# Bucketed attention and a gated MLP on one core: the penalty of unequal buckets from bits and their complements instead of one-hot columns, with the first batch planned anew

## The chip, the core and the metric

The kernel runs on one core of a Trainium2 chip. A core has TensorE (PE, with its weight loads shown as PEld), VectorE (DVE), ScalarE (ACT), GpSimd (POOL) and SyncE (SP), which here issues all DMAs. The metric is the device time of one execution in microseconds. Three runs of the kernel before took 945.35, 940.81 and 940.45 us; their median, 940.81 us, is the time before.

## The reference

Attention over 4 batches, 8 heads, 768 positions and 64 dimensions, in which a query sees only the keys of its own hash bucket, and then a gated MLP without a nonlinearity:

```python
q_bits = (np.einsum('bhsd,dk->bhsk', q, proj) > 0).astype(np.int64)      # proj is 64 x 6
k_bits = (np.einsum('bhsd,dk->bhsk', k, proj) > 0).astype(np.int64)
powers = 2 ** np.arange(n_bits)
q_bucket = np.sum(q_bits * powers, axis=-1)                               # 0 to 63
k_bucket = np.sum(k_bits * powers, axis=-1)
mask = q_bucket[:, :, :, None] == k_bucket[:, :, None, :]
scores = np.where(mask, scale * np.matmul(q, k.transpose(0, 1, 3, 2)), -1e9)
attn = np.exp(scores - np.max(scores, axis=-1, keepdims=True))
attn = attn / (np.sum(attn, axis=-1, keepdims=True) + 1e-09)
x = np.matmul(attn, v) as rows of 512 (8 heads x 64), 3072 rows in all
out = (x @ w_a) * (x @ w_b) @ w_out                                       # 512 -> 1536 -> 512
```

## The kernel before

All matmuls of values run on pairs of 16-bit parts: a number is split into a high part and a remainder, and a product is the sum of three products of parts.

**The blocks of K and Q.** `split` (line 377) prepares one block: K of a pair of heads (12 groups of 128 positions, 16 blocks in all, 4 per batch) or Q of four heads and a third of the positions (8 groups, 24 blocks, 6 per batch). It scales the block, makes the high part (L344 on ACT or L346 on DVE) and the remainder (L402, DVE), which go into tile `pt[0]` (`kt`, `qt`) and through a DMA transpose (L409) into half 1 of the transposed tile `trk` or `trq`. The high part is copied into tile `pt[1]` (L337). PE multiplies the transposed block with `proj` in two parts (L421, 12 columns per group), ACT copies one part out as `neg` (L439), and DVE compares the other with it, which gives six bits per position (L442). A scan (L443) makes the bucket's number from the six bits by Horner's rule. POOL subtracts the number from a table `buckets` of 0 to 63 (L451), and DVE compares the 64 differences with zero (L459): for Q a column holds 2^15 where the number is equal and else 0, for K −2^15 where it is not equal and else 0. The second transpose (L467) brings `pt[1]`, 64 columns of the high part and 64 of these, into half 0.

**Scores.** For each tile of 128 queries and one head, `scores` (L752) adds two products of 128 rows into two blocks of 384 keys: half 0 of Q with half 0 of K, and half 1 with half 1. The 64 one-hot rows add 0 where the buckets are equal and −2^30 where they are not. There are 192 such tiles. DVE takes the maximum (L772) and two small steps (L779, L783), ACT the exponential with its sum (L792), ACT or DVE cast it to 16 bits (L337, into `a`), POOL (or, for tiles whose key is below `BOTH_LO`, DVE) makes the remainder (L340), a DMA transpose (L812) gives `at`, and PE multiplies it with V in 18 matmuls (L821). After eight tiles DVE divides by the sums (L852, tile `x`), and the result is transposed into `xT`, in the first unit by PE (L887) and L893, L896.

**The MLP.** A unit is 256 positions of a batch, 12 units in all. For each of 12 blocks f of 128 of the 1536 columns PE does 24 matmuls (L932, `ab`), ACT scales one half (L947, `a`), DVE multiplies the other with it (L955, `g`), ACT and POOL split the product (L962, L965), and PE does six matmuls with `w_out` (L975, `o`).

**The weights.** They are loaded as 32-bit words and put together anew for 16-bit use, in the first quarter of the run: two ACT steps (L506, L514), one DVE step (L524, `raw_w` or `wo_y`), a cast to the high part (L337 on ACT or DVE), and a remainder (L340 on DVE or POOL) into `wab` or `wo`. A group of weights also needs its maximum (L546) and a scale (L569 to L577).

**The order.** `Plan` records every operation with its engines, an estimated duration, a key, and what it reads and writes. `issue` (line 138) walks through time with these estimates, gives each free engine the ready operation with the least key, chooses the engine where two are allowed, and so writes each engine's order, which is then fixed: an engine does its instructions in that order, each as soon as what it needs is there. Keys count tiles of scores. Those of the first batch are numbers of a table (`FIRST_K`, `FIRST_Q`, `FIRST_V`, `FIRST_X`, `FIRST_W` and so on, lines 45 to 51), those of later ones follow from leads and lags (lines 52 to 54). A tag of buffers limits how many of its tiles live at a time: `two` has 8 tiles (`NTWO`), of which at most two are `pt[0]`, two `pt[1]`, four hold `a`, and one `x2`.

Of the kernel before, what the change touches and what calls it, by code (L numbers as in the profile page):

```python
# [44 lines left out]
FIRST_K = (-16.3, -2.05, -0.08, 1.27)  # L45
FIRST_Q = (-9.7, 0.61)
FIRST_V = (-20.84, -4.29, 0.05, 2.68)
FIRST_X = -16.49
FIRST_W = (5.89, 12.41, 13.69, -22.11, -8.59, 22.86)
FIRST_WO = (6.46, 13.88, 17.5, 26.83, 32.86, -20.47)  # L50
FIRST_M = (20.33, 2.62)
K_LEAD, K_STEP, Q_LEAD, V_LEAD, V_STEP, X_LAG = 7.99, -2.55, 6.99, 5.66, 5.82, 11.54
BOTH_LO = 12.62
M_LAG, E_LEAD, O_LAG = 5.88, 13.29, 3.51
# [9 lines left out]
def constants():  # L64


    c = np.zeros((P, P + NK * NBITS), np.float32)
    c[:, :P] = np.eye(P)
    c[:, P:] = np.tile([0.0] + [2.0] * (NBITS - 1), NK)
    return c, np.tile(np.arange(NBUCK), (P, 1)).astype(np.float16)  # L70

# [166 lines left out]
def attention_moe(ctx: ExitStack, tc: tile.TileContext, q, k, v, proj, w_a, w_b, w_out, cst, cst_w, out):  # L238
# [43 lines left out]
    csb = cp.tile([P, P + NK * NBITS], F32, tag="csb", name="csb")  # L282
    ident = csb[:, :P]
    horner = csb[:, P:]
    buckets = cp.tile([P, NBUCK], F16, tag="buckets", name="buckets")
# [90 lines left out]

    def split(raw, x, n, side, b, key, toks, tag, fast):

# [62 lines left out]
        def numbers():  # L441
            nc.vector.tensor_tensor(out=six(bits), in0=cols(0), in1=six(neg), op=ALU.is_gt)  # L442
            nc.vector.tensor_tensor_scan(  # L443
                out=neg.t[:, :nb], data0=horner[:, :nb], data1=bits.t[:, :nb], initial=0.0,
                op0=ALU.mult, op1=ALU.add,
            )

        op("DVE", 0.6, numbers, key, r=[psb, neg, "csb"], w=[bits, neg], sbuf=True)
        op(
            "POOL", 0.2 + 1.7e-3 * size,  # L450
            lambda: nc.gpsimd.tensor_tensor(  # L451
                out=hot(), in0=buckets.unsqueeze(1).to_broadcast([P, n, NBUCK]),
                in1=six(neg)[:, :, NBITS - 1 :].to_broadcast([P, n, NBUCK]), op=ALU.subtract,
            ),
            key, r=[neg, "buckets"], w=[(pt[1], "hot")],
        )
        op(
            "DVE", 0.18 + 0.25e-3 * size,
            lambda: nc.vector.tensor_scalar(  # L459
# [604 lines left out]
```

## Time and profile before

| | us |
|---|---|
| median of three runs | 940.81 |
| lowest, highest run | 940.45, 945.35 |
| profiled execution, its own time | 945.47 |
| its span, first to last instruction | 943.7 |
| busy in the span: PE, PEld | 863.1, 695.1 |
| busy: DVE, ACT, POOL | 617.9, 607.9, 521.1 |
| DMA: 152.10 MB | 161 GB/s in the mean |

A row of the profile names the line, the engine, the operation and what is written and read (`mx<-s`: a tile `mx` from a tile `s`; buffer numbers are left out). "x192" is the count of instructions. "Busy" is time in which an engine executes; waiting, semaphores and the issuing of DMAs are not counted. The granted clock is the share of TensorE's full clock that it was given in a stretch. The share of the DMA engines is their busy time by the length of the stretch, with transfers that overlap counted apart, so that it can pass 1.

### The profile page before, as it was taken

The page shows a single profiled execution, that of the slowest core. Times are in us where ns is not written, and L with a number is a line of the kernel's source. Part 1 is how long each engine was busy: PE and PEld are TensorE (multiplying, and loading weights), DVE is VectorE, ACT ScalarE, POOL GpSimd, SP SyncE. Part 2 cuts the span into 40 slices and gives each one's busy share as a digit, 9 for nine tenths or more (in the row PEclk, how much of TensorE's full clock was granted, in tenths as well). Part 3 has the DMA queues.
Part 4 walks back from the last instruction along what each step waited for, and adds up shares of the span by engine and source line. Part 5 has one row for each costly group of instructions (what it writes and reads, how often), then busy time and mean ns, then how long its engine had stood idle before and what let it go on. Part 6 is the DMA issues. An engine that isn't in the chain of part 4 may idle for free.

```text
span 943.7 us, 23025 instructions
## 1 busy us (share of the span) xinstructions
PE 863.1 (91%) x9025; PEld 695.1 (74%) x9025; DVE 617.9 (65%) x1508; ACT 607.9 (64%) x1161; POOL 521.1 (55%) x400
## 2 busy tenths in 40 slices
PE   1356578899999999999999999999999999999998
PEld 0234456678888888888888888887888888888886
DVE  5999987978676666557776665567667665543111
ACT  5788678786765766656765776657765766654221
POOL 0345454686756566656666666656565756654111
PEclk9997588999999999999999999999999999999999
DMA  8999989589999687868997787879876777654000
GB/s 264 287 209 231 263 228 201 119 158 223 186 186 167 133 155 173 142 147 183 172 209 142 129 183 144 141 152 190 191 179 112 158 154 136 140 115 88 12 24 23
DMA packets 455725, 152.10 MB, mean 161 GB/s; under 512 B 427328, under 2 KB 447936, under 8 KB 455616
## 3 DMA queue, kind: packets, MB, share of 16 engines
q1 hardware_dynamic: 455616, 150.64, 76.4%
q8 instruction: 70, 1.15, 0.5%
q14 instruction: 39, 0.32, 0.1%
HBM read 37.87 MB, written 6.29 MB: 47 GB/s over the span
## 4 chain that ended last, share of the span: by engine, by line
PE 82%; DVE 9%; DMA 4%; issue 2%; ACT 1%; POOL 1%; SPq 1%; DVEq 0%; ACTq 0%; POOLq 0%
PE ab L932 39%; PE o L975 20%; PE s L752 11%; PE av L821 10%; DMA at<-a 2%; DVE mx L772 2%; DMA raw_w<-in_moe_w_a_dram 1%; DVE raw_w L524 1%; DVE wo_y L524 1%; DMA trq<-qt 1%; DVE wmx L546 0%; DVE wo L340 0%; ACT e L792 0%; DVE wab L340 0%; DVE sc L779 0%
## 5 line engine op out<-in xcount | busy, mean ns | idle before, releaser
L340 POOL TENSOR_TENSOR a<-e,a 128x768 f16<-128x768 f32 x188 | 323.7, 1723 | 204.7 <-ACT a L337 117.4
L932 PE MATMUL ab<-xT,wab 128*128 128x256 f16 x3456 | 418.9, 276 | 5.5 <-DVE g L955 5.4
L932 PEld LDWEIGHTS <-wab 128*128 128x128 f16 x3456 | 332.3, 99 | 64.1 <-issue 17.7
L772 DVE TENSOR_REDUCE mx<-s 128x1 f32<-128x768 f32 x192 | 182.9, 953 | 114.7 <-PE s L752 112.6
L792 ACT ACTIVATE e<-s,bias,sc 128x768 f32<-128x768 f32 x192 | 189.9, 989 | 100.0 <-DVE bias L783 90.7
L975 PE MATMUL o<-wo,g 128*128 128x512 f32 x864 | 237.6, 411 | 0.0
L965 POOL TENSOR_TENSOR g<-g,g 128x256 fp32r<-128x256 f32 x144 | 114.1, 792 | 121.1 <-ACT g L962 119.9
L975 PEld LDWEIGHTS o<-wo,g 128*128 128x128 f32 x864 | 154.6, 189 | 30.0
L752 PE MATMUL s<-trk,trq 128*128 128x384 f16 x768 | 162.8, 343 | 14.9 <-DMA trq<-qt 7.0
L821 PEld LDWEIGHTS <-at 128*128 128x128 f16 x3456 | 127.3, 100 | 42.6 <-DMA at<-a 20.4
L821 PE MATMUL av<-vh,at 128*128 128x64 f16 x2304 | 133.9, 196 | 15.9 <-DMA at<-a 13.1
L955 DVE SCALAR_TENSOR_TENSOR g<-ab,absc,a 128x256 f32<-128x256 f32 x144 | 69.0, 479 | 120.5 <-ACT a L947 75.3
L947 ACT ACTIVATE a<-ab,absc 128x256 f32<-128x256 f32 x144 | 68.2, 473 | 110.9 <-PE ab L932 106.8
L752 PEld LDWEIGHTS <-trq 128*128 128x128 f16 x768 | 70.5, 102 | 60.8 <-issue 25.9
L337 ACT CAST a<-e 128x768 f16<-128x768 f32 x137 | 113.3, 827 | 1.6
L962 ACT CAST g<-g 128x256 fp32r<-128x256 f32 x144 | 58.2, 404 | 60.8 <-DVE g L955 50.7
L821 PE MATMUL av<-vl,at 128*128 128x64 f16 x1152 | 67.3, 196 | 0.0
L451 POOL TENSOR_TENSOR kt<-buckets,neg_k 128x768 f16<-128x768 f16 x16 | 25.4, 1585 | 46.7 <-DVE neg_k L443 26.5
L337 DVE CAST a<-e 128x768 f16<-128x768 f32 x55 | 36.9, 671 | 17.2 <-ACT e L792 17.1
L783 DVE TENSOR_SCALAR bias<-mx,sc 128x1 f32<-128x1 f32 x192 | 41.1, 214 | 6.8
L779 DVE TENSOR_SCALAR sc<-mx,cq 128x1 f32<-128x1 f32 x192 | 40.5, 211 | 4.9
L451 POOL TENSOR_TENSOR qt<-buckets,neg_q 128x512 f16<-128x512 f16 x24 | 30.2, 1256 | 14.9 <-DVE neg_q L443 8.1
(112 smaller groups left out, 643.2 us busy)
## 6 DMA issues: line engine op xcount, KB each, us to landing
vr<-in_v_dram SPq DMA_DIRECT2D x16, 384.0 KB, 4.1
rk<-in_k_dram SPq DMA_DIRECT2D x16, 384.0 KB, 4.2
rq<-in_q_dram SPq DMA_DIRECT2D x24, 256.0 KB, 3.4
raw_w<-in_moe_w_a_dram SPq DMA_DIRECT2D x12, 512.0 KB, 6.3
raw_w<-in_moe_w_b_dram SPq DMA_DIRECT2D x12, 512.0 KB, 5.6
raw_wo<-in_moe_w_out_dram SPq DMA_DIRECT2D x12, 512.0 KB, 5.5
out_dram<-osb SPq DMA_DIRECT2D x24, 256.0 KB, 2.3
at<-a SPq DMA_TRANSPOSE x192, 3.6
```

The source lines that it names most:

```text
L337: (nc.scalar.copy if e == "ACT" else nc.vector.tensor_copy)(out=out, in_=x)
L340: (nc.gpsimd if e == "POOL" else nc.vector).tensor_tensor(out=out, in0=x, in1=y, op=ALU.subtract)
L752: nc.tensor.matmul(ps.t[:, jj, :HALF], lhsT=trq.t[:, i, (2 * j + h) * TPC + t], rhs=tr.t[:, i, k0 : k0 + NT // 2].rearrange("p n s -> p (n ...
L772: lambda: nc.vector.tensor_reduce(out=mx.t[:, col], in_=halves(ps.t), axis=AX.XY, op=ALU.max, negate=True),
L792: lambda: nc.scalar.activation(flat2(e.t), halves(ps.t), AF.Exp, bias=bias.t[:, col], scale=sc.t[:, col], accum_out=sm.t[:, u : u + 1],),
L821: nc.tensor.matmul(av.t[:, u, :], lhsT=at.t[:, a + kt, :], rhs=w.t[:, h, kt, :], start=i == 0, stop=i == 3 * NT - 1,)
L932: nc.tensor.matmul(pl.t[:, m, :CH], lhsT=wt(m, wi, cc, f), rhs=xt.t[:, cc // 2, xi, cc % 2 * TPC : (cc % 2 + 1) * TPC, :], start=i == 0, s ...
L947: lambda a=a, pl=pl, gr=gr: nc.scalar.activation(a.t, pl.t[:, 0, :CH], AF.Copy, scale=absc[:, b, gr : gr + 1]),
L955: lambda a=a, g32=g32, pl=pl, gr=gr: nc.vector.scalar_tensor_tensor(out=g32.t, in0=pl.t[:, 1, :CH], scalar=absc[:, b, gr + 1 : gr + 2], in ...
L962: op("ACT", 0.41, lambda g=g, g32=g32: nc.scalar.copy(out=g[0].t, in_=g32.t), kf - E_LEAD, r=[g32], w=[g[0], "order_g0"])
L965: lambda g=g, g32=g32: nc.gpsimd.tensor_tensor(out=g[1].t, in0=g32.t, in1=f32(g[0].t), op=ALU.subtract),
L975: nc.tensor.matmul(po.t[:, u, :], lhsT=g[gi].t[:, us], rhs=wo_t(f)[:, wi * DM : (wi + 1) * DM], start=f == 0 and i == 0, stop=f == NF - 1 ...
```

## The change

The 64 one-hot columns are replaced by 12 columns. For K they hold −2^15 times the six bits, and then −2^15 times their complements; for Q 2^15 times the complements, and then 2^15 times the bits. Their product sums −2^30 for each bit in which the two differ, so 0 where the buckets are equal. The scan, POOL's subtraction and DVE's comparison over 64 columns are gone, and with them the constants `horner` and `buckets` and their loads. Two DVE operations (`pairs`) write the 12 columns instead.

The rows of half 0 that count are now 64 + 12 = 76 (`NROW`), and `scores` uses only these rows in its first pair of matmuls. The other 52 columns of `pt[1]` have to hold finite numbers, since the transposes take whole tiles: the two `pt[1]` tiles are now fixed (`hp0` and `hp1`, a ring from which `Buf` takes and gives back), and POOL clears their last 52 columns once at the start. `NTWO` goes from 8 to 6. The tables of keys of the first batch, the leads and lags, and `BOTH_LO` have new numbers; with them each engine's order changes throughout.

```diff
-NBUCK = 1 << NBITS
+NROW = D + 2 * NBITS
-NF3, NTWO, NAT, NO = 7, 8, 3, 2
+NF3, NTWO, NAT, NO = 7, 6, 3, 2
-FIRST_K = (-16.3, -2.05, -0.08, 1.27)
+FIRST_K = (-17.68, -1.77, -0.5, 3.12)
-FIRST_W = (5.89, 12.41, 13.69, -22.11, -8.59, 22.86)
+FIRST_W = (8.64, 12.71, 13.7, -33.75, -4.8, 22.98)
...
-BOTH_LO = 12.62
+BOTH_LO = 6.46
...
+            if self.ring is not None:
+                self.real = self.ring.pop(0)
+                return self.real
...
+                        if b.ring is not None:
+                            b.ring.append(b.real)
...
-    op("SP", DMA_ISSUE, lambda: nc.sync.dma_start(out=buckets, in_=cst_w), -60, w=["buckets"], svc=0.1)
...
+    ring = [cp.tile([P, 2 * S], F16, tag=f"hp{i}", name=f"hp{i}") for i in range(NPREP)]
+    for i in range(NPREP):
+        op(
+            "POOL", 0.6,
+            lambda i=i: nc.gpsimd.memset(
+                ring[i].rearrange("p (n a) -> p n a", a=P)[:, :, NROW:], 0.0
+            ),
+            -90, w=["hp"],
+        )
...
-        pt = [two(f"{which}t{i}_{x}", (f"prep{i}", NPREP)) for i in range(2)]
+        pt = [
+            two(f"{which}t0_{x}", ("prep0", NPREP)),
+            Buf(plan, p2, "hp", NPREP, [P, 2 * S], F16, f"{which}t1_{x}", None, ring),
+        ]
...
-        def numbers():
-            nc.vector.tensor_tensor(out=six(bits), in0=cols(0), in1=six(neg), op=ALU.is_gt)
-            nc.vector.tensor_tensor_scan(
-                out=neg.t[:, :nb], data0=horner[:, :nb], data1=bits.t[:, :nb], initial=0.0,
-                op0=ALU.mult, op1=ALU.add,
-            )
...
-            lambda: nc.gpsimd.tensor_tensor(
-                out=hot(), in0=buckets.unsqueeze(1).to_broadcast([P, n, NBUCK]),
-                in1=six(neg)[:, :, NBITS - 1 :].to_broadcast([P, n, NBUCK]), op=ALU.subtract,
-            ),
...
-            lambda: nc.vector.tensor_scalar(
-                out=hot(), in0=hot(), scalar1=0.0, scalar2=(-PEN, PEN)[side],
-                op0=(ALU.not_equal, ALU.is_equal)[side], op1=ALU.mult,
-            ),
...
+            "DVE", 0.2, lambda: nc.vector.tensor_tensor(out=six(bits), in0=cols(0), in1=six(neg), op=ALU.is_gt),
...
+        def pairs():
+            one, other = ((hot()[:, :, i * NBITS : (i + 1) * NBITS]) for i in (side, 1 - side))
+            nc.vector.tensor_scalar(
+                out=one, in0=six(bits), scalar1=(-PEN, PEN)[side], scalar2=None, op0=ALU.mult
+            )
+            nc.vector.tensor_scalar(
+                out=other, in0=six(bits), scalar1=1.0, scalar2=(PEN, -PEN)[side], op0=ALU.subtract, op1=ALU.mult
+            )
...
             for i in range(2):
+                rows = slice(0, (NROW, P)[i])
...
-                        ps.t[:, jj, :HALF], lhsT=trq.t[:, i, (2 * j + h) * TPC + t],
-                        rhs=tr.t[:, i, k0 : k0 + NT // 2].rearrange("p n s -> p (n s)"),
+                        ps.t[:, jj, :HALF], lhsT=trq.t[rows, i, (2 * j + h) * TPC + t],
+                        rhs=tr.t[rows, i, k0 : k0 + NT // 2].rearrange("p n s -> p (n s)"),
```

How the order moved is shown at three places, with the program's own buffer numbers. The line numbers of the changed kernel are its own: L529 there is L524 before, L339 is L340, L336 is L337, L778 is L772, L961 is L955.

The first place is DVE around the first K and Q blocks, before the first tile of scores. Before the change:

```order
L524 SCALAR_TENSOR_TENSOR raw_w_112<-raw_w_112 128x1024
L459 TENSOR_SCALAR kt_0_0_182<-kt_0_0_182 128x12x64
L442 TENSOR_TENSOR bits_q_0_0_275<-qb_0_0_253,neg_q_0_0_264 128x48
L443 SCALAR_TENSOR_TENSOR neg_q_0_0_264<-csb,bits_q_0_0_275 128x48
L337 CAST wab<-raw_w_112 128x2x512
L322 TENSOR_SCALAR po_k_1_283<-ps_k_1_281 128x1
L323 TENSOR_SCALAR po_k_1_285<-po_k_1_283 128x1
L328 TENSOR_SCALAR al_k_1_287<-po_k_1_285 128x1
L328 TENSOR_SCALAR inv_k_1_289<-po_k_1_285 128x1
L763 TENSOR_SCALAR cq_0_0_188<-inv_q_0_0_180,inv_k_1_289 128x1
L340 TENSOR_TENSOR wab<-raw_w_112,wab 128x2x512
L459 TENSOR_SCALAR qt_0_0_0_190<-qt_0_0_0_190 128x8x64
```

The same place with the change, where `hp` is the fixed tile:

```order
L456 TENSOR_TENSOR bits_k_0_250<-kb_0_232,neg_k_0_247 128x72
L462 TENSOR_SCALAR hp_74<-bits_k_0_250 128x12x6
L465 TENSOR_SCALAR hp_74<-bits_k_0_250 128x12x6
L529 SCALAR_TENSOR_TENSOR raw_w_114<-raw_w_114 128x1024
L336 CAST wab<-raw_w_114 128x2x512
L456 TENSOR_TENSOR bits_q_0_0_272<-qb_0_0_254,neg_q_0_0_266 128x48
L462 TENSOR_SCALAR hp_75<-bits_q_0_0_272 128x8x6
L465 TENSOR_SCALAR hp_75<-bits_q_0_0_272 128x8x6
L339 TENSOR_TENSOR wab<-raw_w_114,wab 128x2x512
```

The K block is finished ahead of the first weight word instead of behind it, and the Q block ahead of the weight remainder (1.2 us on DVE) and five small operations instead of behind them.

The second place is POOL, which works on the eight tiles of the first half unit (`a_0_0_0` ...) and the next. Before the change:

```order
L451 TENSOR_TENSOR qt_0_0_1_500<-buckets,neg_q_0_1_536 128x8x64
L340 TENSOR_TENSOR a_0_0_0_1_0_0_624<-e_0_0_1_0_0_588,a_0_0_0_1_0_0_624 128x768
L340 TENSOR_TENSOR a_0_0_0_1_0_1_658<-e_0_0_1_0_1_604,a_0_0_0_1_0_1_658 128x768
L451 TENSOR_TENSOR kt_0_3_572<-buckets,neg_k_3_707 128x12x64
L340 TENSOR_TENSOR a_0_0_0_1_1_0_723<-e_0_0_1_1_0_709,a_0_0_0_1_1_0_723 128x768
L340 TENSOR_TENSOR a_0_0_1_0_0_0_794<-e_0_1_0_0_0_768,a_0_0_1_0_0_0_794 128x768
L340 TENSOR_TENSOR wab<-raw_w_184,wab 128x2x512
L340 TENSOR_TENSOR a_0_0_1_0_0_1_843<-e_0_1_0_0_1_811,a_0_0_1_0_0_1_843 128x768
```

With the change:

```order
L339 TENSOR_TENSOR a_0_0_0_1_0_0_619<-e_0_0_1_0_0_609,a_0_0_0_1_0_0_619 128x768
L339 TENSOR_TENSOR a_0_0_0_1_0_1_640<-e_0_0_1_0_1_626,a_0_0_0_1_0_1_640 128x768
L339 TENSOR_TENSOR a_0_0_0_1_1_0_668<-e_0_0_1_1_0_646,a_0_0_0_1_1_0_668 128x768
L339 TENSOR_TENSOR a_0_0_0_1_1_1_693<-e_0_0_1_1_1_686,a_0_0_0_1_1_1_693 128x768
L339 TENSOR_TENSOR wab<-raw_w_185,wab 128x2x512
L339 TENSOR_TENSOR wab<-raw_w_293,wab 128x2x512
L339 TENSOR_TENSOR wab<-raw_w_227,wab 128x2x512
L339 TENSOR_TENSOR a_0_0_1_0_0_0_889<-e_0_1_0_0_0_878,a_0_0_1_0_0_0_889 128x768
```

In the place of the one-hot blocks stand remainders of the weights, three of them in a row, and all eight remainders of the exponentials of the half unit, of which DVE made three before (`a_0_0_0_1_1_1` is the last of them). Counted over all rows ahead of the fifth product of the first MLP unit (L955, L961), POOL has 25 remainders of exponentials and 9 of weights where it had 20 and 5, and no one-hot blocks where it had 8; DVE has no remainder of exponentials and 3 of weights where it had 4 and 7, 4 weight casts where it had 1, 2 copies of Q blocks where it had none, and 5 casts of exponentials where it had 8. On DVE 26 tiles have their maximum there instead of 25, and 8 half words of `w_out` are put together instead of 6. On PE, 26 tiles of scores and 23 products with V stand ahead of the fifth step's `ab` instead of 25 and 21.

The third place is DVE from the second half unit's `x` to the first product `g` of the first MLP unit. Before, 23 instructions stand between the two; these are the first:

```order
L852 TENSOR_TENSOR x_0_1_1261<-av_0_1_916,r_0_1_950 128x512
L772 TENSOR_REDUCE mx_1_0_1177<-s_1_0_0_0_1_1181 128x1
L779 TENSOR_SCALAR sc_1_0_1188<-mx_1_0_1177,cq_1_0_841 128x1
L783 TENSOR_SCALAR bias_1_0_1190<-mx_1_0_1177,sc_1_0_1188 128x1
L402 SCALAR_TENSOR_TENSOR qt_0_1_1_680<-rq_1_1_574,al_q_1_1_1152,qt_0_1_1_680 128x8x64
L896 TENSOR_TENSOR xT_0_941<-px_0_1_1266,xT_0_941 128x512
L772 TENSOR_REDUCE mx_1_0_1177<-s_1_0_0_1_0_1221 128x1
L569 TENSOR_REDUCE wal_1302<-ps_w_1284 128x1
```

With the change the whole stretch is:

```order
L858 TENSOR_TENSOR x_0_1_1317<-av_0_1_977,r_0_1_975 128x512
L778 TENSOR_REDUCE mx_1_0_1135<-s_1_0_1_0_0_1309 128x1
L785 TENSOR_SCALAR sc_1_0_1157<-mx_1_0_1135,cq_1_0_769 128x1
L789 TENSOR_SCALAR bias_1_0_1159<-mx_1_0_1135,sc_1_0_1157 128x1
L778 TENSOR_REDUCE mx_1_0_1135<-s_1_0_1_0_1_1321 128x1
L902 TENSOR_TENSOR xT_0_907<-px_0_1_1327,xT_0_907 128x512
L785 TENSOR_SCALAR sc_1_0_1157<-mx_1_0_1135,cq_1_0_769 128x1
L789 TENSOR_SCALAR bias_1_0_1159<-mx_1_0_1135,sc_1_0_1157 128x1
L551 TENSOR_REDUCE wmx_1305<-raw_w_1129 128x1
L778 TENSOR_REDUCE mx_1_0_1135<-s_1_0_1_1_0_1402 128x1
L961 SCALAR_TENSOR_TENSOR g_0_0_1419<-ab_0_0_1367,absc,a_0_0_1410 128x256
```

Tiles of the next unit and the weight words that filled the stretch before now stand ahead of `x`: before, the second tile of the next unit's first half is the first with its maximum behind `x`, now it is the fifth.

More of the change, by code (lines that the diff above doesn't have):

```diff
@@ L42 @@
 NRAW, NPREP, NEXP, NA2 = 3, 2, 4, 4
[L45 to L54 removed]
+FIRST_K = (-17.68, -1.77, -0.5, 3.12)
+FIRST_Q = (-6.09, 0.44)
+FIRST_V = (-19.75, -3.23, -2.65, -1.35)
+FIRST_X = -28.17
+FIRST_W = (8.64, 12.71, 13.7, -33.75, -4.8, 22.98)
+FIRST_WO = (2.84, 11.18, 15.86, 25.05, 31.7, -24.67)
+FIRST_M = (18.21, 1.88)
+K_LEAD, K_STEP, Q_LEAD, V_LEAD, V_STEP, X_LAG = 9.01, -3.18, 8.42, 5.66, 5.81, 10.68
+BOTH_LO = 6.46
+M_LAG, E_LEAD, O_LAG = 6.29, 17.05, 3.89
 PEN = float(2.0**15)
@@ L64, in constants @@
 def constants():
[L67 to L70, printed above, removed]
+    return (np.eye(P, dtype=np.float32),)
 HOP = 0.2
@@ L83, with __init__ @@
 class Buf:
-    def __init__(self, plan, pool, tag, bufs, shape, dtype, name, share=None):
+    def __init__(self, plan, pool, tag, bufs, shape, dtype, name, share=None, ring=None):
+        self.ring = ring
         self.plan, self.pool, self.tag, self.bufs = plan, pool, tag, bufs
@@ L237, in attention_moe @@
 @with_exitstack
-def attention_moe(ctx: ExitStack, tc: tile.TileContext, q, k, v, proj, w_a, w_b, w_out, cst, cst_w, out):
+def attention_moe(ctx: ExitStack, tc: tile.TileContext, q, k, v, proj, w_a, w_b, w_out, cst, out):
     nc = tc.nc
@@ L280, in attention_moe @@
     NSTG = 4
[L282 to L285, printed above, removed]
+    ident = cp.tile([P, P], F32, tag="ident", name="ident")
     pj = cp.tile([P, NBITS], F32, tag="pj", name="pj")
@@ L293, in attention_moe @@
     wab16 = wab.bitcast(F16)
-    op("SP", DMA_ISSUE, lambda: nc.sync.dma_start(out=csb, in_=cst), -90, w=["csb"], svc=0.3)
+    op("SP", DMA_ISSUE, lambda: nc.sync.dma_start(out=ident, in_=cst), -90, w=["csb"], svc=0.1)
     for h in range(2):
@@ L439, in split @@
         op("ACT", 0.26, lambda: nc.scalar.copy(out=six(neg), in_=cols(1)), key, r=[psb], w=[neg])
-        def numbers():
-            nc.vector.tensor_tensor(out=six(bits), in0=cols(0), in1=six(neg), op=ALU.is_gt)
-            nc.vector.tensor_tensor_scan(
-                out=neg.t[:, :nb], data0=horner[:, :nb], data1=bits.t[:, :nb], initial=0.0,
-                op0=ALU.mult, op1=ALU.add,
-            )
[L448 to L451, printed above, removed]
-                out=hot(), in0=buckets.unsqueeze(1).to_broadcast([P, n, NBUCK]),
-                in1=six(neg)[:, :, NBITS - 1 :].to_broadcast([P, n, NBUCK]), op=ALU.subtract,
-            ),
-            key, r=[neg, "buckets"], w=[(pt[1], "hot")],
-        )
-        op(
-            "DVE", 0.18 + 0.25e-3 * size,
-            lambda: nc.vector.tensor_scalar(
-                out=hot(), in0=hot(), scalar1=0.0, scalar2=(-PEN, PEN)[side],
-                op0=(ALU.not_equal, ALU.is_equal)[side], op1=ALU.mult,
-            ),
-            key, r=[(pt[1], "hot")], w=[(pt[1], "hot")], sbuf=True,
-        )
+        op(
+            "DVE", 0.2, lambda: nc.vector.tensor_tensor(out=six(bits), in0=cols(0), in1=six(neg), op=ALU.is_gt),
+            key, r=[psb, neg], w=[bits],
+        )
[3 more added lines that the diff above has]
+                out=one, in0=six(bits), scalar1=(-PEN, PEN)[side], scalar2=None, op0=ALU.mult
+            )
+            nc.vector.tensor_scalar(
+                out=other, in0=six(bits), scalar1=1.0, scalar2=(PEN, -PEN)[side], op0=ALU.subtract, op1=ALU.mult
+            )
+        op("DVE", 0.3, pairs, key, r=[bits], w=[(pt[1], "hot")], sbuf=True)
         op(
```

2 lines of the change are left out of this document (1 added, 1 removed).

## The prediction

> **What bounds the kernel now.** I read the busy slices of the page first, then the sums over five stretches, then the chain of waits of the first 125 us, and then single groups. In the slices each digit is a fortieth of the span, 23.6 us:
>
> ```profile
> PE   1356578899999999999999999999999999999998
> PEclk9997588999999999999999999999999999999999
> ```
>
> PE (TensorE) is full from about the ninth slice to the end and half empty before it. The stretches, with length, then busy time and instructions of PE, its weight loads, DVE, ACT and POOL, then granted clock, share of the DMA engines and GB/s:
>
> ```profile
> 0.00:44.00 44.00, 10.13 (x74) 5.73 (x74) 32.51 (x91) 27.59 (x48) 8.23 (x9) 1.00 0.96 278
> 44.00:157.00 113.00, 74.81 (x725) 54.15 (x726) 104.15 (x221) 90.33 (x139) 54.47 (x31) 0.80 1.01 223
> 157.00:212.00 55.00, 51.51 (x516) 40.21 (x516) 44.07 (x86) 44.64 (x81) 39.95 (x28) 0.92 0.75 159
> 212.00:900.00 688.00, 687.36 (x7439) 563.02 (x7438) 431.16 (x1103) 437.03 (x876) 411.23 (x322) 1.00 0.76 152
> 900.00:943.70 43.70, 39.25 (x277) 31.95 (x274) 6.07 (x13) 8.33 (x19) 7.26 (x10) 1.00 0.07 25
> ```
>
> PE is idle for 33.9, 38.2, 3.5, 0.6 and 4.5 us in them, 80.6 us together. From 212 us it waits for nothing, so an instruction saved on another engine there is worth nothing: only what shortens the first 157 us can shorten the run, and after that the same PE work follows. Between 44 and 157 us DVE (VectorE) is busy for 104.15 of 113 us, 92%; ACT for 80%, POOL for 48%. **DVE bounds the filling**, and so I count DVE's work ahead of a fixed point. For that I take the end of the fourth tile's maximum (about 44.0 us) and the end of the fifth product of the first MoE unit (L955, about 156.9 us). Both are on DVE:
>
> ```profile
> 43.06 0.95 DVE L772 TENSOR_REDUCE mx<-s 128x1 f32<-128x768 f32 x1
> 156.45 0.48 DVE L955 SCALAR_TENSOR_TENSOR g<-ab,absc,a 128x256 f32<-128x256 f32 x1
> ```
>
> **DVE's work ahead of the fifth product.** The rows of one line and operation give least, median and largest duration in ns; I use medians.
>
> ```profile
> L443 DVE TENSOR_TENSOR_SCAN neg_q<-csb,bits_q x24: 257/259/1571, 24.2 to 813.1; 128x48 f32<-128x48 f32 x24
> L443 DVE TENSOR_TENSOR_SCAN neg_k<-csb,bits_k x16: 307/308/861, 20.8 to 692.0; 128x72 f32<-128x72 f32 x16
> L459 DVE TENSOR_SCALAR qt<-qt x24: 280/283/826, 27.0 to 815.6; 128x512 f16<-128x512 f16 x24
> L459 DVE TENSOR_SCALAR kt<-kt x16: 348/393/1596, 23.7 to 696.2; 128x768 f16<-128x768 f16 x16
> L442 DVE TENSOR_TENSOR bits_q<-qb,neg_q x24: 193/198/208, 24.0 to 812.9; 128x48 f32<-128x48 f32 x24
> L340 DVE TENSOR_TENSOR a<-e,a x4: 934/939/947, 41.3 to 82.6; 128x768 f16<-128x768 f32 x4
> L340 DVE TENSOR_TENSOR wab<-raw_w,wab x7: 1211/1218/2659, 25.8 to 153.8; 128x1024 f16<-128x1024 f32 x7
> L337 DVE CAST wab<-raw_w x1: 670/670/670, 24.4 to 24.4; 128x1024 f16<-128x1024 f32 x1
> L337 DVE COPY qt<-qt x2: 818/820/822, 433.2 to 639.6; 128x512 f16<-128x512 f16 x2
> L346 DVE TENSOR_SCALAR vh<-vr,al_v x3: 612/620/1228, 8.5 to 233.4; 128x768 f16<-128x768 f32 x3
> L337 DVE CAST a<-e x55: 528/554/2322, 55.6 to 864.7; 128x768 f16<-128x768 f32 x55
> L772 DVE TENSOR_REDUCE mx<-s x192: 906/957/961, 33.9 to 861.8; 128x1 f32<-128x768 f32 x192
> L779 DVE TENSOR_SCALAR sc<-mx,cq x192: 157/214/216, 34.9 to 863.0; 128x1 f32<-128x1 f32 x192
> L524 DVE SCALAR_TENSOR_TENSOR wo_y<-raw_wo x12: 676/689/2141, 132.4 to 186.8; 128x512 int32<-128x512 int32 x12
> ```
>
> Removed with the one-hot columns, for four K and four Q blocks ahead of that point: 4 x 0.308 + 4 x 0.259 for the scans and 4 x 0.393 + 4 x 0.283 for the comparisons, 4.97 us. In their place stand 16 small operations that write six columns per block. No run shows them; the nearest row is the comparison that makes the bits (L442, 0.198), so 0.2 each, 3.2 us. At the ends, 0.16 (the least of L779) and 0.28 (L459), they cost 2.6 to 4.5. Net −1.8 us, so the replacement alone is small.
>
> The new order moves more. From DVE to POOL go four remainders of the exponentials (4 x 0.939) and four of the seven weight remainders (4 x 1.218): −8.6 us. From ACT to DVE come three weight casts (3 x 0.67), two Q copies (2 x 0.82) and two scalings (at most 2 x 0.62): +4.9. From DVE to ACT go three casts of exponentials (3 x 0.554): −1.7. In the changed order one tile more has had its maximum and its two small steps (0.957 + 2 x 0.214), and two weight words more are put together (2 x 0.689): +2.8. The sum is −1.8 − 8.6 + 4.9 − 1.7 + 2.8 = −4.4 us of DVE work; at 92% busy, the fifth product stands **4.8 us earlier**.
>
> **PE's work ahead of it.** PE has also done more by the fifth step: 26 tiles of scores instead of 25, 23 products with V instead of 21. Their prices are from rows in the full stretch, by the distance of their starts:
>
> ```profile
> 555.73 0.34 PE L821 MATMUL av<-vh,at 128*128 128x64 f16 x6
> ...
> 556.26 0.81 PE L752 MATMUL s<-trk,trq 128*128 128x384 f16 x4
> ...
> 556.94 1.65 PE L975 MATMUL o<-wo,g 128*128 128x512 f32 x6
> ```
>
> 0.53 for a product with V, 0.68 for a tile of scores: 0.68 + 2 x 0.53 = **1.7 us** of PE work that need not follow later.
>
> **What is late next.** The first MoE unit needs the attention output of both halves (x), its transposes on PE, 24 matmuls and ACT before DVE's first product:
>
> ```profile
> 21.55 2.28 DVE raw_w L524
> ...
> 27.57 4.83 DMA trq<-qt
> ...
> 100.42 7.34 DMA at<-a
> ...
> 108.98 0.70 DVE x L852
> ...
> 113.73 5.02 PE ab L932 x24
> ...
> 123.68 0.41 DVE g L955
> ...
> 335.05 2.62 PE ab L932 x24
> ```
>
> From x to the end of the first 24 matmuls is 113.73 + 5.02 − 108.98 = 9.8 us. Before, 23 DVE instructions stood between x and the first product and filled this. Now nine stand there: three maxima (2.9), four small (0.9), and two that I price like a maximum (1.9), 5.6 us, at 92% 6.1. DVE takes its rows in order, so behind the waiting product stand the next tiles' scales, and behind those ACT's exponentials. The wait is 0 to 3.7 us; I take the middle, **1.8 us lost**, since in the 9.8 other PE work is included that may stand elsewhere.
>
> **A stall that goes.** The first word of weights took 2.28 us at 21.55; its usual price and what POOL did at that time:
>
> ```profile
> L524 DVE SCALAR_TENSOR_TENSOR raw_w<-raw_w x12: 1168/1216/2664, 21.5 to 155.3; 128x1024 int32<-128x1024 int32 x12
> L451 POOL TENSOR_TENSOR kt<-buckets,neg_k x16: 1489/1492/2053, 21.2 to 692.4; 128x768 f16<-128x768 f16 x16
> ```
>
> POOL's first one-hot block ran just then; it is gone, and POOL has nothing there: **1.0 us** back, and the first Q block's transpose, issued at 27.57 behind the same operations, can go out some 3 us earlier. I count nothing for the latter, since DVE's work up to the fourth tile is the same within 0.3 us.
>
> **Nothing** I put for the rest. POOL's two clears of 624 columns each are priced by its dearest row of 768 columns, 1.65 us (L340, below), 3.3 us together; they stand at the very start, where POOL had nothing before 21.2 us, and the first copy into these tiles came at 11.7:
>
> ```profile
> L337 ACT COPY kt<-kt x14: 821/827/832, 11.7 to 672.6; 128x768 f16<-128x768 f16 x14
> ```
>
> Were they late, that copy would wait for them. The constants loaded shrink by 52 KB. In the blocks after 212 us all is hidden under PE. The first matmul pair of a tile now takes 76 rows instead of 128, with the same number of instructions and columns. No run shows such a matmul. If time went with rows, 192 x 0.34 x 52/128 = 26 us would be gained; if its weight loads stopped running under other matmuls, 384 x 0.098 = 38 us would be lost (the weight load's median is in this row):
>
> ```profile
> L752 PEld LDWEIGHTS <-trq x768: 95/98/152, 32.4 to 861.2; 128*128 128x128 f16 x192
> ```
>
> What the trace does show is that time follows columns: 0.029 for 64, 0.109 for 256 (2.62 / 24), 0.17 for 384, at 128 rows each. So 0 it is, with 1 in 100 for either end.
>
> **Sum.** 4.8 + 1.7 − 1.8 + 1.0 = 5.7 us. The profiled execution took 945.47 us with a span of 943.7, so it would be 939.8 with a span of 938.0. The three runs are 945.35, 940.81 and 940.45; the profiled one is like the slowest of them. From the median of 940.81, **935.1 us**. About 0.5%, 4.7 us, is what a measurement of this kernel can tell from no change.
>
> **Rivals.**
>
> Denser filling, faster by more. In 44 to 157 us the granted clock was 0.80: 15 of 74.8 busy us are lost to it, and 24 matmuls took 5.02 us at 113.73 against 2.62 later. If products and tiles come more evenly, the clock may stand at 0.85 (3.7 us) and the 3.5 idle us of 157 to 212 may go: 940.8 − 5.7 − 3.7 − 3.5 = 927.9. Against it: the same first wait for x, and nothing in the order that aims at PE's gaps.
>
> Transfers instead of DVE. The DMA engines' share is 1.01 in the same stretch, and the chain holds a transpose of 7.34 us at 100.42. The change moves no bytes. If these waits end last wherever DVE is freed, only the stall's 1.0 us stays: 939.8. Against it: DVE was 92% busy, so most waits for transfers were hidden behind it.
>
> POOL holds DVE up, slower than before. Ahead of the fifth product POOL loses eight one-hot blocks and gains five remainders of exponentials and four of weights:
>
> ```profile
> L451 POOL TENSOR_TENSOR qt<-buckets,neg_q x24: 1049/1062/1748, 24.6 to 814.4; 128x512 f16<-128x512 f16 x24
> L340 POOL TENSOR_TENSOR a<-e,a x188: 1631/1647/4153, 38.4 to 865.3; 128x768 f16<-128x768 f32 x188
> L340 POOL TENSOR_TENSOR wab<-raw_w,wab x5: 2122/2135/2149, 69.5 to 157.8; 128x1024 f16<-128x1024 f32 x5
> ```
>
> 5 x 1.647 + 4 x 2.135 − 4 x 1.492 − 4 x 1.062 = 6.6 us more. The largest durations of DVE's rows (2.66 for 1.22, 2.32 for 0.55, 1.60 for 0.39) show what one such meeting costs. Were all 6.6 us paid by DVE, and the wait for x at its upper end (1.9 more), 5.7 − 6.6 − 1.9 = −2.8: 943.6 us. It decides against the change once DVE pays more than 3.8 of the 6.6 us with the late x, or 5.7 without. The Trainium skill ("SBUF — State Buffer", section "Who interferes with whom") states that VectorE and GpSimd share one port pair, held for a whole instruction, the other blocked fully; by that rule each added POOL operation can hold up DVE. The trace agrees at 21.55, where 1.22 us became 2.28. For it: three weight remainders stand in a row on POOL. Against it: POOL is busy 48% and the removed operations met DVE as well.
>
> **How the numbers follow.** Forecast (932 to 938.5) 0.50; transfers 0.23; denser 0.15; POOL 0.10; the 76 rows 0.02. The range leaves out the far part of the denser case, the far part of POOL's and the ends of the 76 rows, not 2 in 10 together: 926 to 943. Faster by over 0.5% is below 936.1: two thirds of the forecast, the denser case and one end of the rows, 0.49. Slower by over 0.5% is above 945.5: a part of POOL's case and the other end, 0.05. The remaining 0.46 is within 0.5%.
>
> **What would show it.** Right: PE idle in the first 212 us falls from 75.6 to about 70, no other change after; the fifth product ends near 153 us (156.9 − 4.8 + 1.8 − 1.0); no first-word row over 1.3 us near 21 us; the tile of scores stays at 0.68 us between starts. Wrong: scores longer or shorter than that; DVE's share in 44 to 153 us well below 92% (transfers); many DVE rows of twice their median (POOL); PE idle in the full stretch (later batches' new lead times too short); a granted clock that moved by more than 0.05.

## The result, and the profile after

The changed kernel takes 931.02 us (median of four runs, 929.26 to 934.97) against 941.42 for the kernel before: a ratio of 0.9888, 95% interval 0.9845 to 0.993, so faster by 0.7 to 1.55%. Measured again beside later experiments it took 930.46 us, 0.9859 [0.9833, 0.9884]. The forecast of 935.1 lay 4.1 us too high, inside its range of 926 to 943.

The profiled execution is the slowest of the four: 934.97 us with a span of 933.2, 10.5 less than before. Its slices, PE and the granted clock:

```profile
PE   1456787999999999999999999999999999999998
PEclk9965599999999999999999999999999999999999
```

PE reaches nine tenths in the eighth slice, from 163 us, where before it did in the ninth, from 189. The same five stretches as in the prediction, with length, PE, its weight loads, DVE, ACT, POOL, granted clock, share of the DMA engines, GB/s:

```profile
0.00:44.00 44.00, 11.85 (x79) 6.96 (x80) 31.37 (x102) 28.34 (x50) 6.82 (x10) 1.00 0.93 283
44.00:157.00 113.00, 78.12 (x758) 55.87 (x758) 101.52 (x213) 90.92 (x141) 62.41 (x37) 0.73 1.07 243
157.00:212.00 55.00, 54.82 (x611) 44.40 (x610) 47.51 (x106) 43.23 (x83) 31.79 (x24) 1.00 0.91 159
212.00:900.00 688.00, 688.00 (x7383) 562.13 (x7381) 417.62 (x1094) 426.39 (x861) 358.18 (x284) 1.00 0.82 149
900.00:933.20 33.20, 28.69 (x200) 23.30 (x198) 4.67 (x9) 6.09 (x14) 5.82 (x8) 0.97 0.04 16
```

PE is idle for 32.2, 34.9, 0.2, 0.0 and 4.5 us: 71.7 in all against 80.6. The third row holds the surprise. Between 157 and 212 us it ran 516 matmuls before and 611 now, at a clock of 0.92 before and 1.00 now. So I followed five points through the traces (ends on DVE, us; x is the attention output of a half unit, the products are those of the MLP, which the prediction calls MoE, L955 before and L961 after). The rows from e2 on belong to experiments that come below:

| run | second x | third x | fifth product | twelfth product | span |
|---|---|---|---|---|---|
| before | 109.7 | 173.2 | 156.9 | 206.5 | 943.7 |
| change | 115.8 | 159.9 | 152.9 | 195.5 | 933.2 |
| change again (e8) | 113.6 | 155.7 | 149.4 | 190.6 | 929.0 |
| new operations, old order (e2) | 110.4 | 171.7 | 156.3 | 205.4 | 942.2 |
| new operations, old table (e5) | 106.5 | 151.1 | 147.3 | 192.2 | 941.5 |
| old FIRST lines (e10) | 109.3 | 169.3 | 150.3 | 200.9 | 941.3 |
| new FIRST lines, the rest of the table old (e12) | 112.5 | 151.8 | 148.0 | 192.2 | 933.8 |

The fifth product came where the forecast put it, 4.0 us earlier. But the twelfth came 11.0 earlier, and only from there on is the distance to the end the same in these two traces (737.2 and 737.7). Priced by the median distance of their starts in the full stretch, the matmuls between the fifth and the twelfth product are 41.0 us of work before and 40.3 after. Before took 49.6 us for them, the change 42.6: **8.6 us lost there before, 2.3 now.** Where before lost them, in rows of the same form:

```profile
153.60:156.60 3.00, 0.07 (x1) 0.00 (x0) 2.96 (x7) 1.94 (x4) 0.00 (x0) 0.91 0.21 49
156.60:162.30 5.70, 5.67 (x33) 4.04 (x33) 1.62 (x4) 3.10 (x5) 4.41 (x3) 0.50 1.01 259
162.30:167.00 4.70, 4.70 (x44) 3.52 (x43) 4.05 (x8) 4.63 (x8) 3.02 (x3) 0.94 1.08 271
167.00:170.50 3.50, 3.50 (x24) 2.58 (x21) 3.43 (x6) 2.06 (x3) 1.04 (x2) 1.00 0.73 112
170.50:173.30 2.80, 0.04 (x1) 0.02 (x1) 2.80 (x4) 2.06 (x5) 1.78 (x1) 0.97 0.00 0
173.30:178.00 4.70, 4.69 (x54) 3.64 (x55) 4.66 (x7) 4.06 (x8) 3.03 (x3) 0.66 0.62 140
```

PE stands for 3.0 us ahead of the fifth product's end, then runs 5.7 us at half the clock, stands again for 2.8 us until the third x is there, and runs 4.7 us at 0.66. Cut where the clock changes, it is 0.50 from 156.1 to 162.9 us and from 173.1 to 176.5 us, and 1.00 between. The first gap lies ahead of the point from which the 8.6 us are counted. Behind it PE is idle for 3.5 us (2.8 of them in the second gap), and the half clock costs 4.7: 8.2 of the 8.6. In the change these are 0.2 and 1.7.

In both gaps DVE is busy throughout (2.96 and 2.80), and the third x, for which PE waits in the second, stands behind a cast of `w_out`:

```profile
170.70 1.87 DVE L337 CAST wo<-wo_y 128x512 fp32r<-128x512 f32 x1
172.48 0.68 DVE L852 TENSOR_TENSOR x<-av,r 128x512 f32<-128x512 f32 x1
```

So DVE's filling work (the weights and first blocks that have to be ready before PE can run without waits) reached past the fifth product, and behind the gaps stands a slow clock whose time counts as busy.

### The profile page after: what moved, and what is told of

Same layout as the page of the kernel before. It is cut to its first block, busy times and chain, and to the rows that moved or that the text cites. A ratio compares the mean times of both kernels' runs of the same rounds, so it can differ in the third digit from the quotient of the medians.

```text
span 933.2 us, 22961 instructions
## 1 busy us (share of the span) xinstructions
PE 861.5 (92%) x9025; PEld 692.7 (74%) x9025; DVE 602.7 (65%) x1521; ACT 595.0 (64%) x1148; POOL 465.0 (50%) x362
## 3 DMA queue, kind: packets, MB, share of 16 engines
q8 instruction: 70, 1.15, 0.5%
## 4 chain that ended last, share of the span: by engine, by line
PE 83%; DVE 6%; DMA 5%; ACT 2%; issue 2%; SPq 2%; POOL 0%; DVEq 0%; ACTq 0%; POOLq 0%
PE ab L938 39%; PE o L981 21%; PE s L758 12%; PE av L827 10%; DMA raw_wo<-in_moe_w_out_dram 1%; DVE mx L778 1%; DMA trq<-hp 1%; DMA raw_w<-in_moe_w_a_dram 1%; DMA raw_w<-in_moe_w_b_dram 1%; DVE raw_w L529 1%; SPq L472 1%; DVE wmx L551 1%; DMA trk<-hp 0%; PE qb L435 0%; SPq L499 0%
## 5 line engine op out<-in xcount | busy, mean ns | idle before, releaser
L339 POOL TENSOR_TENSOR a<-e,a 128x768 f16<-128x768 f32 x192 | 323.1, 1684 | 218.7 <-ACT a L336 119.4
L938 PE MATMUL ab<-xT,wab 128*128 128x256 f16 x3456 | 412.1, 273 | 7.9 <-DVE g L961 7.7
L938 PEld LDWEIGHTS <-wab 128*128 128x128 f16 x3456 | 327.5, 98 | 63.6 <-issue 17.6
L778 DVE TENSOR_REDUCE mx<-s 128x1 f32<-128x768 f32 x192 | 182.7, 952 | 111.2 <-PE s L758 108.3
L971 POOL TENSOR_TENSOR g<-g,g 128x256 fp32r<-128x256 f32 x144 | 111.3, 773 | 190.6 <-ACT g L968 190.3
L758 PE MATMUL s<-trk,trq 76*128 76x384 f16 (+1 forms) x768 | 164.4, 346 | 15.9 <-ACT e L798 11.8
L961 DVE SCALAR_TENSOR_TENSOR g<-ab,absc,a 128x256 f32<-128x256 f32 x144 | 69.1, 480 | 101.9 <-ACT a L953 50.9
L758 PEld LDWEIGHTS <-trq 76*128 76x128 f16 (+1 forms) x768 | 72.4, 102 | 67.3 <-issue 33.4
L336 ACT CAST a<-e 128x768 f16<-128x768 f32 x131 | 108.3, 828 | 2.2
L336 DVE CAST a<-e 128x768 f16<-128x768 f32 x61 | 38.8, 637 | 20.4 <-ACT e L798 19.6
L339 POOL TENSOR_TENSOR wab<-raw_w,wab 128x1024 f16<-128x1024 f32 x9 | 20.0, 2232 | 44.4 <-ACT wab L336 42.8
L798 ACT ACTIVATION_READ_ACCUMULATOR e<-s,bias,sc 128x1 f32 x192 | 37.0, 193 | 0.0
```

The source lines that it names most:

```text
L336: (nc.scalar.copy if e == "ACT" else nc.vector.tensor_copy)(out=out, in_=x)
L339: (nc.gpsimd if e == "POOL" else nc.vector).tensor_tensor(out=out, in0=x, in1=y, op=ALU.subtract)
L758: nc.tensor.matmul(ps.t[:, jj, :HALF], lhsT=trq.t[rows, i, (2 * j + h) * TPC + t], rhs=tr.t[rows, i, k0 : k0 + NT // 2].rearrange("p n s - ...
L778: lambda: nc.vector.tensor_reduce(out=mx.t[:, col], in_=halves(ps.t), axis=AX.XY, op=ALU.max, negate=True),
L798: lambda: nc.scalar.activation(flat2(e.t), halves(ps.t), AF.Exp, bias=bias.t[:, col], scale=sc.t[:, col], accum_out=sm.t[:, u : u + 1],),
L938: nc.tensor.matmul(pl.t[:, m, :CH], lhsT=wt(m, wi, cc, f), rhs=xt.t[:, cc // 2, xi, cc % 2 * TPC : (cc % 2 + 1) * TPC, :], start=i == 0, s ...
```

## Experiments

The ratios are to the kernel before, run beside each set of experiments. Its median was 941.4 to 943.4 us in these sets, so medians of different sets compare to within some 2 us.

### The matmuls of 76 rows (e1)

```diff
-                rows = slice(0, (NROW, P)[i])
+                rows = slice(0, P)
```

> The changed kernel in its own order, but with all 128 rows in the first matmul pair of each tile of scores (the 52 rows more are zeros). By both theories of the gain the row count costs nothing: 931 us, within 2. If PE's time went with rows, the run would be 26 us longer (957); if weight loads of 76 rows did not run under other matmuls, up to 38 us shorter (893).

Measured: 929.14 us, 0.9857 [0.9825, 0.9889]. The groups of scores in the full stretch (name, shape, count, busy us, mean ns), first of the change and then of this run:

```profile
L758 PE MATMUL s<-trk,trq 76*128 76x384 f16 x302 | 74.3, 327 | 0.0
L758 PE MATMUL s<-trk,trq 128*128 128x384 f16 x302 | 73.8, 325 | 0.0
```

```profile
L758 PE MATMUL s<-trk,trq 128*128 128x384 f16 x599 | 117.8, 327 | 0.0
```

76 rows take what 128 take. The zero put for them was right; they are no part of the gain.

### The new operations in the old order (e2)

The kernel before, every instruction in its old place; in each block the scan and the one-hot subtraction go, and two small operations stand where the comparison stood:

```diff
-            nc.vector.tensor_tensor_scan(out=neg.t[:, :nb], ...)
...
-            lambda: nc.gpsimd.tensor_tensor(out=hot(), ...),
+            lambda: None,
...
-            lambda: nc.vector.tensor_scalar(out=hot(), ...),
+            pairs,
```

> The new operations (two of six columns, 76 rows, nothing on POOL) put into the order of before, instruction for instruction: only the penalty's operations differ from before, nothing is moved. Theory A (the gain is DVE work that the new order moved off DVE in the filling): 1.8 us less DVE work at 92% and the stall of 1.0 us, so about 3 us below before, 937 to 940. Theory B (the gain is the shorter chain of the K and Q blocks and POOL's freed time): 8 us or more below before, under 933.5.

Measured: 943.93 us, 1.0006 [0.9983, 1.003]. Both missed: the replacement alone brings nothing. The small operations cost what was put for them; in the trace of the change, with least, median and largest ns:

```profile
L462 DVE TENSOR_SCALAR hp<-bits_q x24: 176/230/1030, 23.7 to 798.2; 128x48 f16<-128x48 f32 x24
L462 DVE TENSOR_SCALAR hp<-bits_k x16: 186/198/1239, 20.9 to 664.2; 128x72 f16<-128x72 f32 x16
```

What the prediction had not seen stands in this run's chain of waits (start, length, what):

```profile
99.98 8.55 DMA at<-a
108.58 1.16 PE av L838 x18
109.76 0.70 DVE x L869
...
153.20 1.14 DVE wab L354
154.56 0.22 DVE bias L800
154.87 1.09 ACT e L809 x2
156.00 0.36 PE qb L438 x8
156.36 5.28 PE ab L949 x24
```

The second x waits for a transpose of exponentials that ends at 108.5 us, against 107.8 before: DVE time saved ahead of it turns into idle time. Up to 110 us DVE is busy for 88.0 us here and for 93.8 before, and yet the second x ends 0.8 us later. Behind it stand the same weight words in the same order, and PE stands and slows at the same place (5.28 us for 24 matmuls, 5.29 before).

### Work put back on DVE, on POOL, and on both (e3, e4, e9), and only later (e7)

The changed kernel, its order kept. e3 puts a scan and a 64-column comparison back on DVE in the ten blocks of the first batch, 4 x (0.308 + 0.393) + 6 x (0.259 + 0.283) = 6.1 us by the rows of before; their results are overwritten or unused. e4 puts 24 subtractions on POOL there, whose results nobody reads and whose medians (0.626 and 0.619) make 14.9 us; e9 has both, e7 both in all later blocks and none in the first batch.

```diff
         def pairs():
+            if b == 0:
+                nc.vector.tensor_tensor_scan(out=neg.t[:, :nb], data0=bits.t[:, :nb], ...)
+                nc.vector.tensor_scalar(out=hot(), in0=hot(), scalar1=0.0, ...)
+                for i in range(n // 4):
+                    nc.gpsimd.tensor_tensor(out=scr..., in0=scr0..., in1=six(bits)..., op=ALU.subtract)
```

> The changed kernel in its own order, with the scan and the comparison over 64 columns put back on DVE in the ten blocks of the first batch (6.0 us of DVE work, 5.0 of it ahead of the fifth product; their results are overwritten). Theory A (DVE's time in the filling is the end's time): 5 to 6.5 us longer than the changed kernel, 936 to 937.5. Theory B (chain and POOL): 0 to 2 us longer, 931 to 933.

> The changed kernel in its own order, with POOL subtractions of the one-hot block's size put back in the ten blocks of the first batch, into a scratch tile nobody waits for (about 13 us of POOL work). Theory A: POOL was busy 55% in the filling, so 0 to 2 us longer, 931 to 933. Theory B, or POOL holding DVE up at the shared port: 5 us longer or more, over 936.

> The changed kernel with both extras in the first batch, the scan and the comparison on DVE and the one-hot subtraction on POOL, as work that nobody waits for; the order is that of the change. Theory A (costs add): 4.9 us for DVE's and 3.0 for POOL's, so 939 when the change is at 931. Theory D' (the two engines' extras meet and cost more together, which alone would explain that the one-hot columns with the new table took 948.6): 944 or more. If it is 939, the rest of the 948.6 comes from the chain DVE, POOL, DVE within a block and from the order that the planner makes of it.

> The changed kernel with the scan, the comparison on DVE and the one-hot subtraction on POOL put back as extra work in every block of K and Q after the first batch, and none in the first batch; the order is that of the change. Theory A (from 212 us on PE waits for nothing, so an instruction more on another engine there is worth nothing): 929 to 934, PE idle after 212 us within 1.5 us of the change. Rival (meetings of DVE and POOL in the full stretch hold PE up): above 936.

| run | median us (lowest to highest) | ratio [95%] |
|---|---|---|
| change again (e8) | 930.46 (929.15 to 930.86) | 0.9859 [0.9833, 0.9884] |
| e3, DVE | 935.93 (935.24 to 936.84) | 0.9939 [0.9916, 0.9963] |
| e4, POOL | 934.04 (931.22 to 936.44) | 0.9915 [0.9886, 0.9945] |
| e9, both | 946.16 (940.49 to 951.54) | 1.0026 [0.9997, 1.0054] |
| e7, both, later | 934.49 (931.04 to 935.55) | 0.9906 [0.9876, 0.9937] |

> The changed kernel itself, unaltered, so that the next three stand beside it on one chip: every theory says 929 to 935, a ratio near 0.989.

In the new order 6.1 us of DVE cost 5.5 us by the medians (against e8) and 7.5 by the ratios, and in the traces the fifth product ends 6.0 us later than in e8: DVE's time in the filling is the run's time. 14.9 us of POOL cost 3.6 or 5.3, between the two theories. Both together cost 15.7, by either. By the medians that is well over the sum, 9.1, and beyond the 944 of theory D'; by the ratios the sum is 12.8, which the intervals do not tell from 15.7. In the profiles up to 160 us, 11 and 14 DVE rows (e8 and the first profile of the change) took over 1.15 times the median of their shape, 15 in e3, 23 in e4 and 28 in e9. In e9 the comparison alone, with least, median and largest ns:

```profile
L473 DVE TENSOR_SCALAR hp<-hp x10: 260/495/1707, 20.8 to 197.3; 128x512 f16<-128x512 f16 x6, 128x768 f16<-128x768 f16 x4
```

Its least is 260, and half of the ten took 495 or more. That the extras cost more together because they meet is argued from such rows, not shown. The profiled run of e9 took 941.61 us, 4.5 less than the median, so a part of the 15.7 us stands in no trace. What the trace has stands early: of 10.8 us of span over e8, 7.9 are there at the second x and 8.4 at the fifth product.

e7 lies half a us above its expectation, 4.0 over e8. Its profile took 692.4 us from the twentieth product to the end, the change's two 690.2 and 691.0, and PE was idle for 1.2 us between 212 and 900 us, where theirs have 0.0 and 0.5. So in the full stretch thirty blocks of the same extras cost 1.4 us (traces) to 4.4 (ratios), in the filling ten blocks cost 15.7.

### The operations and the table of numbers apart (e5, e6)

The changed kernel with the whole table of before, and the kernel before with the table of the change; the planner orders each anew.

> The changed kernel (the small bit operations) with the table of numbers of before: the planner orders the new operations by the old due times. Theory A (the gain comes from the work that the new table takes off DVE in the filling; the replacement alone brings nothing, as its run in the exact old order with 943.9 us against 941.7 showed): 938 to 944, the ratio's interval holds 1.0. Theory B (the shorter chain of K and Q blocks is worth something as soon as the planner may move the rest up behind it): 930 to 935, near the change as a whole.

> The kernel before (64 one-hot columns) with the table of numbers of the change. Theory A, in its strong form (the table alone makes the gain): 6 us of DVE more than the change in the filling, which cost 4.9 us when they were put back alone, and 12 us of POOL more, which cost 3.0 us alone, so 931 + 7.9 = 939, a ratio of 0.997. Theory D (the new table only pays with the room that the small operations leave on DVE and POOL; with the one-hot blocks its later due times collide): above 943, a ratio over 1.002. Below 935 would say that the one-hot columns cost nothing at all.

```diff
-FIRST_K = (-17.68, -1.77, -0.5, 3.12)
+FIRST_K = (-16.3, -2.05, -0.08, 1.27)
...
-M_LAG, E_LEAD, O_LAG = 6.29, 17.05, 3.89
+M_LAG, E_LEAD, O_LAG = 5.88, 13.29, 3.51
```

(e5 against the change; e6 has the same lines the other way round, in the kernel before.)

| | old table | new table |
|---|---|---|
| 64 one-hot columns | 1 | 1.0058 [1.0037, 1.0078] |
| twelve columns of bits | 1.0007 [0.999, 1.0024] | 0.9859 [0.9833, 0.9884] |

Neither half brings anything; the new table with the old operations even loses (948.61 us, theory D). e6 and e9 agree: the new plan with the one-hot work on DVE and POOL is slower than before. So the small operations are worth nothing in the old plan, and 16 (e9) to 18 us (e6) in the new one. (`NTWO` and the fixed tiles go with the operations here.)

The trace of e5 also shows how little an early point says. Its fifth product ends 9.7 us and its third x 22.1 us earlier than before, both earlier than in the change, and yet it takes as long as before. By the same prices it loses 6.9 us from the fifth to the twelfth product and 7.1 from the twelfth to the twentieth, where the change's two traces lose 0.8 to 2.3 and then 0.5. Of the 8.3 us that PE waits between 140 and 260 us, 6.7 are for DVE. Here the part that DVE bounds lasts beyond the twelfth product.

### Which numbers (e10, e11, e12)

```diff
 # e10, against the change: the seven FIRST lines of before
-FIRST_K = (-17.68, -1.77, -0.5, 3.12)
+FIRST_K = (-16.3, -2.05, -0.08, 1.27)
...
 # e11, against the change
-M_LAG, E_LEAD, O_LAG = 6.29, 17.05, 3.89
+M_LAG, E_LEAD, O_LAG = 5.88, 13.29, 3.51
 # e12, against the change: FIRST lines new, all others of before
-BOTH_LO = 6.46
+BOTH_LO = 12.62
...
```

> The changed kernel with only the times of the first batch (the seven FIRST lines) taken back to those of before; the general lead times keep the new values. Theory F (the gain lies in the plan of the first batch): 939 to 945. Theory G (it lies in the general lead times): 929 to 934.

> The changed kernel with only M_LAG, E_LEAD and O_LAG taken back; up to the sixth product DVE's order is that of the change. Theory G (the 6 us that are gained between the fifth and the twelfth product come from the earlier lead of the MoE's elementwise work): the fifth product near 153, the twelfth near 201, 935 to 938. Theory F (they come from the third half unit's x, which the first batch's order already sets): the twelfth near 196, 929 to 933.

> The changed kernel with the new FIRST lines and every other number of the table (the lead times of later blocks, BOTH_LO, M_LAG, E_LEAD, O_LAG) taken back to those of before: the mirror of the run with the old FIRST lines, which took 942.7 us. Theory F (the plan of the first batch makes the gain, together with the small operations): the third x before 162 us, 928 to 934, a ratio of 0.985 to 0.991. Theory H (the first batch's times only pay with the lead times of the second batch's blocks, which stand in the same first 250 us): the third x near 170, above 937.

Measured: e10 942.69 us, 0.9987 [0.997, 1.0003]; e11 929.91, 0.9855 [0.9829, 0.9881]; e12 937.27, 0.9941 [0.9916, 0.9965]. The MoE's leads (e11) do nothing. The plan of the first batch is needed (theory F); that the rest of the table does not matter is wrong: without the other lead times and BOTH_LO over half the gain is gone. Which of these it is stays open. The third x of e12 is early (151.8), as theory F asked, but behind it 4.3 us are lost up to the twelfth product and 2.9 up to the twentieth.

e10 is the sharpest of all. Its fifth product ends at 150.3 us, as early as in the change (152.9, and 149.4 in e8), and yet it takes as long as before. By the reasoning of the prediction it should have been near 931. What DVE does there between the fifth and the sixth product (start, length, instruction):

```profile
149.88 0.47 DVE L961 SCALAR_TENSOR_TENSOR g<-ab,absc,a 128x256 f32<-128x256 f32 x1
...
151.73 1.22 DVE L529 SCALAR_TENSOR_TENSOR raw_w<-raw_w 128x1024 int32<-128x1024 int32 x1
152.86 1.08 DVE L336 CAST a<-e 128x768 f16<-128x768 f32 x1
153.87 2.15 DVE L336 CAST wab<-raw_w 128x1024 f16<-128x1024 f32 x1
155.94 2.00 DVE L336 CAST a<-e 128x768 f16<-128x768 f32 x1
157.86 1.21 DVE L339 TENSOR_TENSOR wab<-raw_w,wab 128x1024 f16<-128x1024 f32 x1
159.00 0.94 DVE L778 TENSOR_REDUCE mx<-s 128x1 f32<-128x768 f32 x1
159.86 0.47 DVE L961 SCALAR_TENSOR_TENSOR g<-ab,absc,a 128x256 f32<-128x256 f32 x1
```

Ten us without a break: the last weights and casts of the filling stand ahead of the sixth product. In the change they are on POOL (nine of the twelve weight remainders, five before and in e10) or done by then. PE in e10 at that time:

```profile
155.00:160.30 5.30, 1.02 (x5) 0.59 (x4) 5.30 (x6) 2.32 (x3) 2.52 (x2) 0.88 0.69 158
160.30:165.60 5.30, 5.22 (x28) 3.63 (x28) 5.16 (x12) 4.62 (x8) 2.33 (x2) 0.50 1.40 290
```

It stands for 4.3 us, and the clock is at half from 159.1 to 165.9 us. From the fifth to the twelfth product e10 takes 50.5 us for some 41.5 us of work. That these DVE rows are what it loses by is read from the trace; no run moves them alone.

## Why the prediction was near, and where it failed

**The fifth product near 153: it ended at 152.9.** The close hit is luck in part, for not all parts of the sum stand, and in the second profile (e8) it ended at 149.4. Of that difference 1.5 us stood already at the fourth product. The other 1.9 are one meeting that the prediction had as its rival on POOL. DVE in the first profile, and POOL at the same time:

```profile
147.82 4.66 DVE L529 SCALAR_TENSOR_TENSOR wo_y<-raw_wo 128x512 int32<-128x512 int32 x2
152.40 0.47 DVE L961 SCALAR_TENSOR_TENSOR g<-ab,absc,a 128x256 f32<-128x256 f32 x1
```

```profile
147.68 1.73 POOL L339 TENSOR_TENSOR a<-e,a 128x768 f16<-128x768 f32 x1 [2.08 <-ACT a L336]
149.38 2.56 POOL L339 TENSOR_TENSOR wab<-raw_w,wab 128x1024 f16<-128x1024 f32 x1
```

Two operations of 0.69 took 4.66 us beside two POOL rows in succession. In the second profile they took 2.74, the latter of them 0.68. The rule that the prediction quoted from the Trainium skill ("SBUF — State Buffer", section "Who interferes with whom"), that one of the two blocks the other for a whole instruction, fits these rows. As a rival it failed on its size: 14.9 us of POOL cost 3.6 to 5.3 (e4), and of the added 6.6 it feared all.

**DVE's work ahead of it, −4.4 us: right in size.** From 44 us to the fifth product DVE is busy for 104.1 us before, for 100.1 with the change and for 96.1 in the second profile, where fewer rows were held up.

**The replacement alone, −1.8 us of DVE: right as a duration, nothing as time** (e2). Ahead of the second x the end was set by the transposes. That is the rival of the transfers, true for the first 108 us of the old order and not for the new one, where e3 showed DVE's time to be the run's.

**The stall of the first weight word, 1.0: right.** The change's row:

```profile
21.61 1.23 DVE L529 SCALAR_TENSOR_TENSOR raw_w<-raw_w 128x1024 int32<-128x1024 int32 x1 [0.45 <-ACT raw_w L519]
```

**The wait for the first x, 1.8 lost: not as put.** The new plan gets the second x 6.1 us later (115.8) and goes from its start to the end of the first product in 7.3 us, where 9.8 had been counted to the end of the matmuls alone; the first product came 1.7 us earlier.

**PE's work ahead, 1.7: 0.4**, by all matmuls up to the fifth product (51.9 against 51.5 us): by then PE has made 23 products with V in both traces, and only one tile of scores more. **The 76 rows, 0: right** (e1). **The clock** in 44 to 157 us was 0.73, and 0.80 in the second profile; the first would have been a sign against the forecast, but the time followed neither.

**The step that failed** is the first one: "only what shortens the first 157 us can shorten the run, and after that the same PE work follows." It took the fifth product for the end of the part that DVE bounds. The 3.5 idle us and the clock of 0.92 in 157 to 212 stood in the prediction's rows and were left as they were. But from the fifth product to the third x 16.2 us passed, in which DVE was busy for 11.4 us with weights, casts and attention, and the gaps that this made on PE were followed by a slow clock. The new plan clears it ahead of time: 7.0 us from the one to the other, 4.1 of them busy, and the third x 13.3 us earlier. So the sum is 4.0 + 0.4 as forecast in kind, and 6.3 between the fifth and the twelfth product, which I had put at 0; 10.7 against 10.5 of span measured. So the time came out near the forecast although the largest part of the gain was put at nothing: the forecast had 5.7 us, the medians differ by 10.4. The denser rival had the 3.5, and its 927.9 lies nearer to the measured 931.0 than the forecast's 935.1; but it put the clock's part into the stretch before 157, where the clock did not rise.

## What to carry to other kernels

Follow an early gain to the last point at which the other engine still makes PE wait, not to a point at which PE first looks full: there 3.5 us of idle PE, with the half clock behind two gaps of about 3 us, made 8.6. An early product or an early x does not prove that this point is passed (e5, e10). A cheaper operation in a fixed order on in-order queues is worth what the next wait leaves of it, which can be nothing, and a plan that needs the room can be worse without it: test the operations and the order in all four combinations. Keep an engine's last filling work from standing ahead of the first product that the bound engine waits for; if it can go to a second engine, price the meetings of the two.
